# A small-matmul shift convolution, accumulating DMAs and regrouped set-up tables in a two-layer sequence-mixing kernel

## The chip, the cores and the metric

The kernel runs on one core of one Trainium2 chip. The metric is the device time of one execution in microseconds (us), and every quoted time is a median of several executions. Executions of one kernel agree within about 1% here (1.4% in e4). Two executions were slow, one of e5 and the profiled one of e15. They enter no ratio, and the medians of these two runs are given with and without them.

A ratio is the mean time of one kernel's fast runs over the mean of the fast runs of the kernel before in the same rounds on the same chip, so it is not quite the ratio of the medians that stand beside it. Intervals are 95%.

PE is the matmul engine (TensorE), PEld its weight load, DVE is VectorE, ACT is ScalarE, POOL is GpSimd, and SP issues DMAs. The granted clock is the share of PE's full clock that the profile shows, from 0 to 1. `L254` in a profile is line 254 of that kernel's own file, so that the same code has another line number in each kernel.

## The reference, cut to what matters

Four residual blocks follow one another on x of 2048 tokens by 640 channels: A, B, A, B, with the same weights in both rounds.

```python
def _A_ref(x, Lambda_re, Lambda_im, B_re, B_im, C_re, C_im, log_dt, Dskip):
    Lam_bar = exp(exp(log_dt) * Lam)                       # complex, 640 states
    B_bar = ((Lam_bar - 1.0) / Lam)[:, None] * Bmat
    h[t] = Lam_bar * h[t-1] + B_bar @ x[t]                 # 2048 steps
    return 2.0 * (h @ Cmat.T).real + x * Dskip

def _B_ref(q, k, v, shift_k, ssm_k, ssm_D):                # does not depend on x
    k_shift = sum over 4 taps of shifted k * shift_k       # per channel
    kv = k_shift * v
    y = irfft(rfft(kv) * rfft(ssm_k))[:2048] + kv * ssm_D  # long convolution
    return q * y

x = x + _A_ref(_layernorm(x), ...)      # layer one:   "A1" in the kernel
x = x + _B_ref(...)                     # layer two:   "B1"
x = x + _A_ref(_layernorm(x), ...)      # layer three: "A2"
x = x + _B_ref(...)                     # layer four:  "B2"
```

(q in B is the normalised x.) The long convolution is done once, by transforms written as matmuls with sine and cosine tables, in five blocks of 128 channels.

## The kernel before: the parts that matter

The kernel is a list of 862 named tasks. A string `ORDER` fixes the order in which they are emitted, and with it the order of each engine's queue: every engine works its own tasks strictly in that order. A suffix chooses an engine where there is a choice (`/a` ACT, `/d` DVE). A table `PLACE` fixes where each buffer lies in one large on-chip array, so that buffers share space over time. Order and places are the product of an earlier search.

```python
for w in ORDER.split():
    nm, _, e = w.partition("/")
    t = by.pop(nm)
    assert all(d.name in done for d in t.deps), nm
    done.add(nm)
    t.emit({"a": "act", "d": "dve"}[e] if e else t.engs[0])
```

PE's results leave the matmul banks by copies, which ACT or DVE performs. There are 174 of them, 145 on ACT and 29 on DVE.

```python
def evac(nc, eng, out, in_):
    if eng == "act":
        nc.scalar.activation(out, in_, ACT.Copy)
    else:
        nc.vector.tensor_copy(out, in_)
```

The shift convolution: diagonal matrices of the taps are the stationary operand, and k streams through in 512 columns. The product with v goes to DRAM and is read back in another layout.

```python
for b in range(2):
    for l in range(4):
        t0 = KPAD + 1024 * h + 512 * b - l
        nc.tensor.matmul(pk[:, 512 * b:512 * (b + 1)], lhsT=s_ds.get()[:, l, :], rhs=kT[:, t0:t0 + 512],
                         start=(l == 0), stop=(l == 3))
...
nc.vector.tensor_tensor(s_vT.get()[:, sl], s_pk.get(), s_vT.get()[:, sl], ALU.mult)
...
nc.sync.dma_start(out=kvd[kb * P:(kb + 1) * P, :], in_=s_vT.get())
```

The residual of layer one: x is loaded a second time and added by an identity matmul at the end of each output tile.

```python
if reload is not None:
    ops = ops + [(ident[:], resid(q)[:, d0:d1], d0, d1)]
```

The set-up: sines and exponentials alternate on ACT, and the negated tables are made on DVE.

```python
def e_p3(_):   # "a_p3": exponential
    nc.scalar.activation(tl("dt", [P, NJ])[:], st["pf"][:, 2, :], ACT.Exp)
...
def e_f3(_):   # "yt_f3": sine
    nc.scalar.activation(part(768, 256), part(768, 256), ACT.Sin, scale=TWO_PI / 32.0)
...
def e_nsi(_):  # "yt_nsi"
    nc.vector.tensor_scalar(T["NSi"].get(), T["Si"].get(), -1.0, None, ALU.mult)
```

## Time and profile before

The time is 352.71 us (351.51 to 353.8).

| quantity, kernel before | value |
|---|---|
| span of the profiled execution | 349.0 us |
| PE / DVE / ACT busy | 325.5 / 328.5 / 241.5 us |
| mean granted PE clock | 0.987 |
| activation table loads | 8 of 1.28 us |

I add one view here: the busy time of each engine in two stretches, the set-up with the long convolution (0 to 140 us) and the rest. The columns are the stretch and its length, busy us (and instructions) of PE, PEld, DVE, ACT and POOL, then the granted clock, the DMA share and GB/s.

```profile
0.00:140.00 140.00, 126.47 (x1766) 102.95 (x1778) 130.40 (x235) 128.20 (x169) 19.34 (x51) 0.99 1.01 198
140.00:340.00 200.00, 198.89 (x1770) 143.07 (x1788) 192.35 (x259) 111.91 (x212) 0.00 (x0) 1.00 0.33 83
```

In the second row PE is full (99%), with DVE next at 96%. In the first row DVE is busy 93% of the time, ACT 92%, PE 90%.

### The profile page before, as it was taken

Reading aid. Unit: us, or ns where it says so; the run is one execution under the profiler, and the core shown is the slowest. Engines: PE = TensorE matmul, PEld = TensorE weight load, DVE = VectorE, ACT = ScalarE, POOL = GpSimd, SP = SyncE. Lnnn points to the kernel's source line nnn. Section 1 sums busy time; section 2 is a strip of 40 time slices with the busy share of each in tenths; the row PEclk is TensorE's granted clock in tenths of the full one; section 3 lists DMA queues with packets and bytes.
Section 4 is the critical chain, followed back from the end, with each engine's and each line's share of the span. In section 5 each row is a group of like instructions: output and inputs, shape, how many; then the busy total and the mean of one; then the engine's idle time right before and its main releaser. Section 6 shows DMA issues by size and latency. Waiting matters only on the chain.

```text
span 349.0 us, 8399 instructions
## 1 busy us (share of the span) xinstructions
PE 325.5 (93%) x3533; PEld 246.0 (70%) x3565; DVE 328.5 (94%) x504; ACT 241.5 (69%) x383; POOL 19.3 (6%) x51
## 2 busy tenths in 40 slices
PE   6669998999999999999999999999999999999990
PEld 6437976777686998896776685686868758755550
DVE  8989899898999999999989999999989989999996
ACT  5999998899899999563585598286317727307561
POOL 7590000000000000000000000000000000000000
PEclk9899999999999999999999999999999999999996
DMA  7999999999999977497067800306064040000204
GB/s 221 210 215 219 150 169 234 213 151 223 217 252 190 201 160 135 97 264 230 30 120 123 289 28 2 75 2 153 0 141 162 2 77 0 2 0 3 82 34 188
DMA packets 118712, 45.91 MB, mean 132 GB/s; under 512 B 111629, under 2 KB 112914, under 8 KB 118674
## 3 DMA queue, kind: packets, MB, share of 16 engines
q1 hardware_dynamic: 118528, 45.36, 60.2%
q8 instruction: 28, 0.46, 0.5%
q14 instruction: 10, 0.08, 0.1%
q10 hardware_dynamic: 146, 0.01, 0.0%
HBM read 17.38 MB, written 7.86 MB: 72 GB/s over the span
## 4 chain that ended last, share of the span: by engine, by line
PE 70%; DVE 19%; ACT 5%; DMA 2%; issue 2%; ACTq 1%; DVEq 0%; SPq 0%
PE banks L726 31%; PE banks L635 11%; PE banks L638 11%; PE banks L470 4%; DVE arena L247 4%; ACT arena L245 3%; PE banks L1162 2%; PE banks L1163 2%; PE banks L1025 2%; DMA arena<-in_A_Dskip_dram 1%; DMA arena<-kvd 1%; DVE arena L1141 1%; DVE arena L1140 1%; DVE arena L1139 1%; DVE arena L1138 1%
## 5 line engine op out<-in xcount | busy, mean ns | idle before, releaser
L245 ACT ACTIVATE arena<-banks 128x1024 bf16<-128x1024 f32 (+4 forms) x145 | 120.5, 903 | 37.1 <-PE banks L638 13.3
L726 PE MATMUL banks<-arena 128*128 128x128 bf16 (+1 forms) x859 | 116.5, 290 | 1.1
L726 PEld LDWEIGHTS <-arena 128*128 128x128 bf16 x880 | 67.8, 98 | 48.3
L638 PE MATMUL banks<-arena 128*128 128x256 bf16 x400 | 56.7, 273 | 0.0
L635 PE MATMUL banks<-arena 128*128 128x256 bf16 x400 | 56.7, 273 | 0.0
L674 DVE TENSOR_TENSOR_SCAN arena<-arena 128x1290 bf16<-128x1290 f32 x16 | 44.6, 2832 | 0.2
L638 PEld LDWEIGHTS <-arena 128*128 128x128 bf16 x400 | 39.1, 98 | 4.5
L635 PEld LDWEIGHTS <-arena 128*128 128x128 bf16 x400 | 38.5, 98 | 4.2
L544 ACT ACTIVATE junk<-arena,nmean 128x640 bf16<-128x640 f32 x48 | 39.6, 826 | 1.3
L1087 PE MATMUL banks<-arena 128*128 128x128 bf16 x170 | 35.1, 219 | 0.6 <-ACT arena L245 0.6
L1090 PE MATMUL banks<-arena 128*128 128x128 bf16 x170 | 35.4, 219 | 0.0
L247 DVE CAST arena<-banks 128x1024 bf16<-128x1024 f32 (+3 forms) x29 | 30.2, 1060 | 2.9 <-PE banks L1092 1.1
L1092 PE MATMUL banks<-arena 128*128 128x128 bf16 x150 | 32.8, 219 | 0.0
L1089 PE MATMUL banks<-arena 128*128 128x128 bf16 x150 | 32.8, 219 | 0.0
L589 ACT ACTIVATE arena<-arena,nmr,rstd 128x640 bf16<-128x640 f32 (+1 forms) x26 | 22.7, 912 | 7.4 <-DVE nmr L556 7.4
L539 ACT ACTIVATE nmean<-sums 128x4 f32<-128x4 f32 (+1 forms) x15 | 3.0, 203 | 31.7 <-DVE arena L738 28.2
L1025 PE MATMUL banks<-arena 128*128 128x512 bf16 x74 | 19.6, 397 | 3.4 <-ACT arena L245 2.9
L734 ACT ACTIVATE arena<-banks 128x640 f32<-128x640 f32 x12 | 8.4, 701 | 19.3 <-PE banks L726 19.3
L1162 PE MATMUL banks<-arena 128*128 128x128 bf16 x160 | 19.6, 219 | 0.5 <-ACT arena L245 0.5
L1163 PE MATMUL banks<-arena 128*128 128x128 bf16 x160 | 19.3, 219 | 0.6 <-DVE arena L1143 0.6
L591 DVE TENSOR_SCALAR arena<-arena,rstd,nmr 128x640 bf16<-128x640 f32 (+1 forms) x34 | 17.3, 543 | 0.1
L1087 PEld LDWEIGHTS <-arena 128*128 128x128 bf16 x170 | 16.6, 98 | 1.1
(201 smaller groups left out, 537.5 us busy)
## 6 DMA issues: line engine op xcount, KB each, us to landing
arena<-in_A_x_dram SPq DMA_DIRECT2D x8, 640.0 KB, 5.4
arena<-ysd SPq DMA_DIRECT2D x8, 640.0 KB, 4.9
arena<-in_B_ssm_k_dram SPq DMA_DIRECT2D x5, 512.0 KB, 6.4
kvd<-arena SPq DMA_DIRECT2D x5, 512.0 KB, 7.4
arena<-kvd SPq DMA_DIRECT2D x5, 512.0 KB, 5.1
ysd<-arena SPq DMA_DIRECT2D x5, 512.0 KB, 4.4
out_dram<-arena SPq DMA_DIRECT2D x8, 320.0 KB, 2.2
arena<-in_A_B_re_dram SPq DMA_DIRECT2D x1, 800.0 KB, 6.3
```

Of the source, the lines that this page charges most:

```text
L245: nc.scalar.activation(out, in_, ACT.Copy)
L247: nc.vector.tensor_copy(out, in_)
L544: nc.scalar.activation(small.junk, src(q), ACT.Square, bias=st["nmean"][:, i:i + 1], scale=1.0, accum_out=st["ssq"][:, i:i + 1])
L635: nc.tensor.matmul(pb[:, jj, c2, :], lhsT=bt1[:, c2, j, k, :], rhs=uT[:, 0:2, k, :], start=(k == 0), stop=False)
L638: nc.tensor.matmul(pb[:, jj, c2, :], lhsT=bt0[:, c2, k, j * P:(j + 1) * P], rhs=uT[:, 2:4, k, :], start=False, stop=(k == NJ - 1))
L674: nc.vector.tensor_tensor_scan(gv, rt, gv, 0.0, ALU.mult, ALU.add)
L726: nc.tensor.matmul(pc[:, o0:o1], lhsT=lh, rhs=rh, start=(n == 0), stop=(n == len(ops) - 1))
L1025: nc.tensor.matmul(pk[:, 512 * b:512 * (b + 1)], lhsT=s_ds.get()[:, l, :], rhs=kT[:, t0:t0 + 512], start=(l == 0), stop=(l == 3))
L1087: nc.tensor.matmul(ps[:, g, 0, :], lhsT=T["Cf"].get()[:, q, :], rhs=are, start=True, stop=single)
L1089: nc.tensor.matmul(ps[:, g, 0, :], lhsT=T["Sf"].get()[:, q, :], rhs=A[:, 2 * q + 1, :], start=False, stop=True)
L1090: nc.tensor.matmul(ps[:, g, 1, :], lhsT=T["NSf"].get()[:, q, :], rhs=are, start=True, stop=single)
L1092: nc.tensor.matmul(ps[:, g, 1, :], lhsT=T["Cf"].get()[:, q, :], rhs=A[:, 2 * q + 1, :], start=False, stop=True)
```

## The change

The change wants to take work from PE (identity matmuls; cheaper convolution), from ACT (table loads) and from DVE (table work to GpSimd, late sums to the DMA), and comes with a new order and new places for everything. Cut to its core:

```diff
-    t0 = KPAD + 1024 * h + 512 * b - l
-    nc.tensor.matmul(pk[:, 512 * b:512 * (b + 1)], lhsT=s_ds.get()[:, l, :], rhs=kT[:, t0:t0 + 512], ...)
+    t0 = KPAD + P * (8 * h + a) - l
+    for r in range(2):
+        rs = slice(64 * r, 64 * (r + 1))
+        nc.tensor.matmul(pk[:, r, a], lhsT=kT[rs, t0:t0 + P], rhs=s_ds.get()[rs, l, rs], ...)
 ...
-            nc.sync.dma_start(out=kvd[kb * P:(kb + 1) * P, :], in_=s_vT.get())
-            nc.sync.dma_start(out=s_xv.get(), in_=rows(kvd[c0:c0 + DQ, :]))
+            nc.sync.dma_start_transpose(out=s_xv.get(), in_=s_kv.get())
 ...
-                    if reload is not None:
-                        ops = ops + [(ident[:], resid(q)[:, d0:d1], d0, d1)]
+                def e_xa(_, q=q, s_p=s_p):
+                    nc.gpsimd.dma_start(out=s_x[q].get(), in_=dram(q) if dram is not None else s_p.get(), accum_op=ALU.add)
 ...
+                        nc.gpsimd.dma_start(out=s_b.get()[:, q, :], in_=s_x[q].get(), accum_op=ALU.add)
 ...
-        nc.vector.tensor_scalar(T["NSi"].get(), T["Si"].get(), -1.0, None, ALU.mult)
+        (nc.vector if eng == "dve" else nc.gpsimd).tensor_scalar(T["NSi"].get(), T["Si"].get(), -1.0, None, ALU.mult)
```

(Cut: the same engine choice for two other negations and the diagonals `a_lamd`; the column tables `yt_h1` on GpSimd; the exponentials `a_p5a` split from the sines `a_p5b`; layer one's batch statistics as four tasks per chunk; the mean of a LayerNorm taken from sums so that it does not wait for the DMA; `ORDER` and `PLACE` entirely new.) In the new order five table tasks carry the suffix `/p`, GpSimd: `yt_neg12`, `yt_neg6`, `a_lamd`, `yt_nsi` and the small `yt_h3`.

## The prediction

> **What bounds the kernel now.** I read the windows table first, with the execution cut at the three places where its character changes, then the page's row of tenths, the chain of waits, the waits of each engine, and last the groups of instructions for durations. The windows table (busy us, with counts, of PE, weight loads, DVE, ACT and POOL, then clock, DMA share and GB/s):
>
> ```profile
> 0.00:26.20 26.20, 17.18 (x169) 12.31 (x172) 22.30 (x65) 22.45 (x32) 18.98 (x48) 0.93 1.00 215
> 26.20:139.60 113.40, 108.89 (x1594) 90.28 (x1602) 107.71 (x170) 105.34 (x137) 0.36 (x4) 1.00 1.02 193
> 139.60:340.20 200.60, 199.41 (x1774) 143.43 (x1792) 192.95 (x260) 112.31 (x212) 0.00 (x0) 1.00 0.33 83
> 340.20:349.00 8.80, 0.00 (x0) 0.00 (x0) 5.56 (x12) 1.42 (x4) 0.00 (x0) 0.68 0.48 186
> ```
>
> PE is busy 325.5 of 349.0 us. Its idle time is 9.0 us in the set-up, 4.5 in the middle, 1.2 in the long late stage and 8.8 in the tail. A busy PE need not be a fast one, so I checked its rate in the chain of waits (start, duration, what):
>
> ```profile
> 136.32 0.55 PE banks L635 x5
> 140.69 0.55 PE banks L1063 x16
> 156.06 0.93 PE banks L1190 x32
> ```
>
> Five matmuls of 256 columns take 0.55 us, 109 ns each, so 1280 columns cost 0.55 us with hardly a gap. From 140 to 340 us the end is set by the number of columns that PE has to stream: a microsecond of matmul removed there is a microsecond gained, as long as DVE, 193 of 200.6 us busy, keeps up. ACT has 88 us free there. In the middle all three engines are 93 to 96% busy, so a gain needs relief on all three.
>
> The set-up is different. Its chain runs through ACT and not through PE:
>
> ```profile
> 12.36 0.68 ACT arena L245
> 13.06 1.28 ACT L319
> 14.56 1.18 ACT arena L245 x2
> 15.76 1.28 ACT L883
> 17.05 0.42 ACT arena L883
> 17.47 1.19 ACT arena L245 x2
> 18.67 1.28 ACT L332
> ...
> 20.28 1.28 ACT L334
> ```
>
> The four pieces of 1.28 us are activation table loads. They alternate exponential, sine, exponential, sine. The chain also shows once what the trip of the product kv through DRAM costs:
>
> ```profile
> 63.18 0.75 SPq L1175
> 64.03 4.24 DMA arena<-kvd
> 68.29 1.30 DVE arena L1138
> ```
>
> **What the Trainium skill says.** (1) "TensorE: Matmul & The Clock Gate", section "Back-to-back issue gap": a warm matmul costs N/2.4 + 2.5 ns, with a floor near 25 ns for small N. The trace agrees on the first: 109 ns at 256 columns, and 29 ns at 64 (32 in 0.93 us). It has nothing smaller to show the floor. (2) "ScalarE activation tables: per-element evaluation and per-set limits", section "What a function is on this engine": two functions of different sets are one table load of 1283 ns apart. The trace has eight loads of 1283 ns. (3) "DMA: Bandwidth & Descriptors", section "SWDGE vs HWDGE vs iDMA": accumulation in a DMA is to be had only from GpSimd's software-generated descriptors; its section on the anatomy of such a DMA fits about 2.0 us plus bytes over 436 GB/s. This kernel issues no DMA from GpSimd, so no trace of before tests it. (4) "SBUF — State Buffer", section "SBUF: two separate sides": GpSimd cannot write descriptors while DVE runs an operation in a two-port mode. This is untested here too.
>
> **The change part by part.**
>
> *Residual of layer one.* In each of 16 output tiles two identity matmuls (512 and 128 columns) that added x are gone, and so are the four second loads of x. PE loses 16 x 640 = 10240 columns; at 0.55 us for 1280 that is 8 x 0.55 = 4.4 us. All of it lies between 159 and 262 us, where PE is the bound: 4.4 us on the path. x is now added by 16 accumulating DMAs of 128x640, each estimated by the skill's fit at 2.0 us plus 0.4 to 0.8 us. They come between the eviction and the sum of squares of the next layer, so they lengthen a chain of dependences, not an engine's work, and the mean no longer waits for them.
>
> *Shift convolution.* Before: 80 matmuls of 512 columns. In the timeline eight start at 60.48 and the next instruction at 62.22, so 217 ns each and 17.4 us in all. After: 640 matmuls of 64 columns with 64 rows, in pairs on the two halves of the rows. How long one takes is the most uncertain number. If the pairs gain nothing, the rate is that of the last transform (29 ns): 18.6 us, a loss of 1.2. But the first transform already uses such half-row pairs: 16 of 128 columns in 0.55 us, 34 ns each where a full-row one takes 55, a factor of 0.62. The same factor on 29 ns gives 18 ns and 11.6 us, a gain of 5.8. With the skill's floor of 25 ns it is 16 us, a gain of 1.4. I take 20 ns: 12.8 us, a gain of 4.6 on PE. The product on DVE (ten of 1.22 us) now reads and writes in runs of four elements; I expect 1.25, no change. The store and reload of kv become one transposing DMA between on-chip buffers: a store of 7.4 us to landing and a load of 5.1 give way to about 5.9 (what such transposes take now).
>
> *Exponentials apart from sines.* In the new order of tasks ACT meets sine, exponential, sine, root: four loads for eight, 4 x 1.28 = 5.1 us of ACT. Two of them are in the chain of the set-up: 2.6 us on the path. Another sits near 127 us, where the chain also ran through ACT.
>
> *Set-up tables.* The little column operations of the last transform's table leave DVE (about 4 us between 11.0 and 15.2), as do the diagonal of lambda (2.3), two negations and the negated sine (1.6); the factor table shrinks by about 1.5. In exchange 5 more evictions of 640 (0.8 each), and about 6 more of 1024 (1.2), are given to DVE, so DVE gains only about nothing to 2 us before 140. ACT gives those evictions away (about 10 us) plus 5.1 of loads and takes two statistics early and two later (some 2.6 each).
>
> *Late sums.* The last additions of two chunks (8 x 0.82 = 6.6 us of DVE) become accumulating DMAs, and five of the 16 additions of layer three leave DVE for ACT evictions (5 x 0.90 = 4.5). With ten fewer normalisations (about 5.3) and four fewer statistics (4.2), less what DVE takes on, DVE falls by some 17 us to about 312 and stops being a near second bound. By itself this is worth little: PE was 99.4% busy beside it.
>
> **Sum.** PE 4.4 + 4.6 = 9.0 us less; set-up idle 2.5 us less (one path, so I do not add DVE's relief); 1 us of new waits for accumulating DMAs; the tail of 8.8 us as it was, since its last chunk is not among those changed. 349.0 - 9.0 - 2.5 + 1.0 = 338.5 us of span. The median stands 3.7 us above the span of this trace: 342.2 us.
>
> **Rivals.** *The accumulating DMAs turn into the wait.* For it: they have to be issued from GpSimd while DVE is busy 96% of the time, in-order ACT then sits in front of a sum of squares, and the next layer's matmuls hang on it. Against it: ACT has 88 us of slack late, it waits now already 28.2 us for additions of DVE without PE starving, and DVE's work falls. If each of the 16 of layer one cost PE half a microsecond, 8 us would be lost and the time would be 350. *The small matmuls are bound by issue or weight loads.* Each now has its own weight load of 128 columns; at 29 ns the gain of 4.6 turns into a loss of 1.2 and the time is 348. *All is hidden but PE's columns:* if the set-up shortens no path, because its end is set by the same DMAs (DMA share 1.00 there), the time is 344.7. *It goes better:* DVE and ACT freed in the middle let PE close its 4.5 us of idle, and the convolution takes the 18 ns: about 337.
>
> **Range and chances.** The sum of the good cases reaches about 336, the one bad case of a rival 348 to 350; 8 times in 10 between 336.0 and 348.5. Two per cent faster is 345.6; three of the four parts would have to fail for the time to be above it, or the DMA rival has to hold. Faster 0.77, within 2% 0.20, slower 0.03.
>
> **What would show it.** PE busy near 316 us; the convolution's ten groups of 64 in about 1.3 us each (1.9 would make the second rival right); four table loads; PE idle before 26 us near 6.5 us; DVE busy near 312; still over 99% PE busy from 140 us to the last matmul. A PE that waits late in the span, with ACT's sums of squares released by a DMA, would make the first rival right and the prediction wrong.

## The result, and the profile after

The changed kernel takes 363.88 us (363.04 to 364.57): ratio 1.0316 [1.0276, 1.0357], 11 us slower where 10.5 us faster was predicted. Its results are correct.

The same two stretches of the changed kernel:

```profile
0.00:140.00 140.00, 113.70 (x2135) 98.37 (x2136) 120.81 (x198) 109.17 (x153) 36.07 (x66) 0.91 0.91 168
140.00:340.00 200.00, 198.01 (x1856) 146.34 (x1854) 181.79 (x230) 125.42 (x226) 23.72 (x27) 1.00 0.56 115
```

The second row still runs at 99% PE, as before. The first row lost 12.8 us of PE's busy time, although the clock there was 0.91, so that a busy microsecond did less. DVE and ACT are less busy as well: 9.6 and 19.0 us. Only GpSimd is busier, 36.1 us for 19.3, and it is far from full. So less was done in the first row because engines wait for one another or for data, and not because one of them is full.

Over the whole span, the first sign that the prediction had named did not come. PE was to be busy near 316 us; the page says

```profile
PE 325.0 (90%) x4093; PEld 252.4 (70%) x4093; DVE 319.9 (88%) x459; ACT 246.4 (68%) x407; POOL 64.2 (18%) x98
```

It was 325.5 before. PE's idle time rose from 23.5 to 37.3 us. Fewer columns were streamed, but up to 90 us the granted clock was 0.87 (0.98 before), and matmuls took longer at a lower clock: a group of 64 of the convolution 1.89 us at 23 us, where the clock was 0.50, and 1.04 us at 92 us, where it was 1.00.

A finer cut of the changed kernel shows where PE stands idle:

```profile
0.00:27.20 27.20, 16.62 (x229) 14.38 (x231) 20.85 (x64) 17.43 (x25) 14.73 (x38) 0.75 0.87 194
27.20:51.80 24.60, 21.00 (x476) 19.42 (x471) 21.26 (x37) 20.37 (x30) 9.90 (x21) 0.93 0.93 154
51.80:68.00 16.20, 8.64 (x119) 8.04 (x118) 15.47 (x9) 9.61 (x15) 11.33 (x7) 0.80 0.64 121
68.00:90.60 22.60, 18.22 (x529) 16.53 (x528) 19.15 (x18) 20.86 (x25) 0.11 (x1) 0.99 0.94 147
```

PE is idle for 10.6, 3.6, 7.6 and 4.4 us in these, 26 us by 90.6 us; before, it was idle for 12.2 us by 90 us (77.8 busy). The first figure was to fall from 9.0 to near 6.5.

Two places stand out in the timeline (start, duration, engine, line, operation, shapes, and in brackets the idle time before and what ended it). At 51 us, POOL first, then DVE:

```profile
50.55 6.79 POOL L882 TENSOR_SCALAR arena<-arena 128x2176 bf16<-128x2176 bf16 x1 [8.38 <-DVE arena L1169]
```

```profile
50.45 1.29 DVE L1170 TENSOR_TENSOR arena<-arena 128x2176 bf16<-128x2176 bf16 x1
51.85 6.40 DVE L1171 TENSOR_TENSOR arena<-arena 128x2176 bf16<-128x2176 bf16 x1
```

The negation `yt_nsi` on GpSimd and a product on DVE overlap. The product has the same shape as the one ahead of it, which took 1.29 us, but takes 6.40 us, and it ends at 58.25 us, shortly after GpSimd's 57.34. GpSimd in turn seems to have got going only when the product at 50.45 had ended, at 51.74; that leaves 5.6 us of its own. PE waits behind it (columns: who waited for whom, us in total, times, longest):

```profile
PE banks L1116 <- DVE arena L252: 6.6, 1, 6.6
```

At 4 us DVE stands still:

```profile
8.30 0.21 DVE L312 CAST arena<-arena 20x128 f32<-20x128 bf16 x1 [4.10 <-DMA arena<-in_A_Dskip_dram]
8.44 0.60 DVE L855 TENSOR_SCALAR arena<-arena,pidx 128x768 int32<-128x768 f32 x1
```

The cast `a_p0` needs a small load that lands at 8.3 us. In the new order it stands ahead of two phase tables that need no load at all, and a queue in order makes those wait.

What the prediction had asked to look at otherwise: the convolution's groups, a line of the chain of waits, and the accumulating DMAs, from the page's table of DMA issues (KB each, us from issue to landing):

```profile
91.65 1.04 PE banks L1056 x64
```

```profile
arena<-in_A_x_dram POOLq DMA_DIRECT2D x16, 320.0 KB, 5.1
arena<-arena POOLq DMA_DIRECT2D x8, 320.0 KB, 5.4
```

### The profile page after: what moved, and what is told of

Its sections match the earlier page's. It is cut to its first block, busy times and chain, and to the rows that moved or that the text cites. A ratio compares the mean times of both kernels' runs of the same rounds, so it can differ in the third digit from the quotient of the medians.

```text
span 362.3 us, 9541 instructions
## 1 busy us (share of the span) xinstructions
PE 325.0 (90%) x4093; PEld 252.4 (70%) x4093; DVE 319.9 (88%) x459; ACT 246.4 (68%) x407; POOL 64.2 (18%) x98
## 4 chain that ended last, share of the span: by engine, by line
PE 44%; DVE 28%; DMA 10%; issue 10%; ACT 7%; POOL 1%; ACTq 1%; DVEq 0%; POOLq 0%
PE banks L737 11%; DMA arena<-arena 7%; PE banks L651 6%; PE banks L654 6%; PE banks L469 4%; DVE arena L252 3%; ACT arena L250 3%; DVE arena L1171 3%; PE banks L1056 3%; PE banks L1193 2%; PE banks L1194 2%; PE banks L1092 2%; PE banks L1116 2%; DMA arena<-in_A_x_dram 2%; ACT junk L546 2%
## 5 line engine op out<-in xcount | busy, mean ns | idle before, releaser
L250 ACT ACTIVATE arena<-banks 128x1024 bf16<-128x1024 f32 (+4 forms) x134 | 114.2, 911 | 38.6 <-PE banks L654 19.9
L737 PE MATMUL banks<-arena 128*128 128x128 bf16 (+1 forms) x880 | 114.8, 292 | 0.7 <-ACT arena L746 0.7
L737 PEld LDWEIGHTS <-arena 128*128 128x128 bf16 x880 | 66.6, 98 | 48.1 <-issue 0.8
L546 ACT ACTIVATE junk<-arena,nmean 128x640 bf16<-128x640 f32 x40 | 33.0, 825 | 27.3 <-DVE nmean L541 11.5
L252 DVE CAST arena<-banks 128x1024 bf16<-128x1024 f32 (+3 forms) x40 | 39.9, 1014 | 8.4 <-PE banks L1121 4.4
L752 POOL DMA_DIRECT2D arena<-in_A_x_dram x16 | 14.1, 962 | 175.4 <-ACT arena L746 147.9
L651 PEld LDWEIGHTS <-arena 128*128 128x128 bf16 x400 | 38.3, 98 | 6.2 <-DMA arena<-arena 1.1
L1116 PE MATMUL banks<-arena 128*128 128x128 bf16 x170 | 35.8, 223 | 7.6 <-DVE arena L252 6.6
L654 PEld LDWEIGHTS <-arena 128*128 128x128 bf16 x400 | 39.1, 98 | 4.5
L1119 PE MATMUL banks<-arena 128*128 128x128 bf16 x170 | 36.2, 223 | 0.0
L599 ACT ACTIVATE arena<-arena,nmr,rstd 128x640 bf16<-128x640 f32 (+1 forms) x35 | 30.8, 911 | 4.5 <-DVE nmr L558 3.7
L1118 PE MATMUL banks<-arena 128*128 128x128 bf16 x150 | 33.3, 222 | 0.0
L1121 PE MATMUL banks<-arena 128*128 128x128 bf16 x150 | 33.3, 222 | 0.0
L746 ACT ACTIVATE arena<-banks 128x640 f32<-128x640 f32 x16 | 11.2, 698 | 20.2 <-PE banks L737 11.8
L1193 PE MATMUL banks<-arena 128*128 128x128 bf16 x160 | 21.2, 228 | 0.7 <-ACT arena L250 0.6
L1194 PE MATMUL banks<-arena 128*128 128x128 bf16 x160 | 21.0, 228 | 0.5 <-DVE arena L1174 0.4
L1118 PEld LDWEIGHTS <-arena 128*128 128x128 bf16 x150 | 15.0, 100 | 8.0 <-issue 7.9
L1116 PEld LDWEIGHTS <-arena 128*128 128x128 bf16 x170 | 16.9, 100 | 0.9
L417 DVE SCALAR_TENSOR_TENSOR arena<-arena,s_F 128x640 bf16<-128x640 bf16 x20 | 17.2, 874 | 0.1
```

Of the source, the lines that this page charges most:

```text
L546: nc.scalar.activation(small.junk, src(q), ACT.Square, bias=st["nmean"][:, i:i + 1], scale=1.0, accum_out=st["ssq"][:, i:i + 1])
L599: nc.scalar.activation(dst, src, ACT.Identity, bias=st["nmr"][:, i:i + 1], scale=st["rstd"][:, i:i + 1])
L651: nc.tensor.matmul(pb[:, jj, c2, :], lhsT=bt1[:, c2, j, k, :], rhs=uT[:, 0:2, k, :], start=(k == 0), stop=False)
L654: nc.tensor.matmul(pb[:, jj, c2, :], lhsT=bt0[:, c2, k, j * P:(j + 1) * P], rhs=uT[:, 2:4, k, :], start=False, stop=(k == NJ - 1))
L737: nc.tensor.matmul(pc[:, o0:o1], lhsT=lh, rhs=rh, start=(n == 0), stop=(n == len(ops) - 1))
L1116: nc.tensor.matmul(ps[:, g, 0, :], lhsT=T["Cf"].get()[:, q, :], rhs=are, start=True, stop=single)
```

## The experiments

Theory one after the first look: the late part gained as predicted, and the set-up lost more by two mistakes of placement, the negation on GpSimd and the early cast. Rival: the new operations themselves cost time, the accumulating DMAs above all. A third possibility came up later: the predicted gains were not on the path to begin with.

### The two waits in the set-up

**e1**, the long negation back on DVE:

```diff
-    ... a_b1e0:2/a yq1_vl yt_nsi/p a_b1e1:2/a ...
+    ... a_b1e0:2/a yq1_vl yt_nsi/d a_b1e1:2/a ...
```

> The changed kernel with one task given back: the negated sine table (128x2176) is made by DVE again and not by GpSimd. Theory 1 (GpSimd's 6.8 us operation holds DVE's two-input multiplication up, 6.40 us for 1.29, and PE starves for 6.6 us behind it and comes back at a lower clock): about 357 us (356 to 359), the long multiplication back at 1.29 us. Theory 2 (the accumulating DMAs are what cost): no change, 363 to 365. Theory 3 (the start is late because DVE waits 4.1 us for a small load): little change, 362 to 364, since that wait lies before.

Measured: 359.13 us, ratio 1.0192 [1.0146, 1.0239], 4.8 us below the changed kernel. The negation now costs DVE 0.72 us and no product is stretched:

```profile
56.39 0.72 DVE L884 TENSOR_SCALAR arena<-arena 128x2176 bf16<-128x2176 bf16 x1
```

**e2**, the cast that needs the late load (and another small task, `kv_d0`) put behind the last phase table:

```diff
-    ... yt_f0 a_p0 yt_ph6 yq0_kl kv_d0 yt_ph0 kv_d1 ...
+    ... yt_f0 yt_ph6 yq0_kl yt_ph0 kv_d0 a_p0 kv_d1 ...
```

> The changed kernel with two small tasks moved in DVE's order: the conversions of the small loads stand after all three phase tables instead of before the last two. Theory 3 (DVE, which takes its tasks in order, waits 4.1 us for a small load that lands at 8.2 us, and the sine tables wait behind it): about 360 us (358.5 to 362), the wait of 4.1 us at most 2. Theory 1 (the port) and theory 2 (the DMAs): 363 to 365.

Measured: 360.44 us, ratio 1.0237 [1.0192, 1.0283], 3.4 us below. DVE's wait for the load fell from 4.10 to 1.39 us:

```profile
8.26 0.21 DVE L314 CAST arena<-arena 20x128 f32<-20x128 bf16 x1 [1.39 <-DMA arena<-in_A_Dskip_dram]
```

**e3**, both edits together:

> Both edits together. If theories 1 and 3 are both right and their gains add: 352 to 355 us, about the kernel before. If the second only moves work into the wait that the first left: no better than the first alone, about 357. If both are wrong: 363 to 365.

Measured: 356.14 us, ratio 1.0095 [1.0042, 1.0147], 7.7 us below. The two nearly add up (4.8 + 3.4 = 8.2), so they are separate losses. The kernel is still slower than before.

**e4**, the reverse test: the kernel before with nothing changed but the long negation on GpSimd.

```diff
-        nc.vector.tensor_scalar(T["NSi"].get(), T["Si"].get(), -1.0, None, ALU.mult)
+        nc.gpsimd.tensor_scalar(T["NSi"].get(), T["Si"].get(), -1.0, None, ALU.mult)
```

> The kernel before with only the negated sine table moved to GpSimd, nothing else. Theory 1: GpSimd takes 6 to 7 us for it, a DVE operation with two inputs beside it is stretched to 3 to 7 us, and the kernel gets slower, 355 to 360 us. Theory 2 or 3: the same as before or a little faster, 351 to 353, as 0.72 us of DVE is saved.

Measured: 358.63 us, ratio 1.0166 [1.01, 1.0232], 6.1 us slower than the kernel before. So the loss needs no new order. Another DVE operation was hit this time, GpSimd first, then DVE:

```profile
38.69 5.71 POOL L856 TENSOR_SCALAR arena<-arena 128x2176 bf16<-128x2176 bf16 x1 [12.28 <-DMA arena<-arena]
```

```profile
38.71 6.13 DVE L418 SCALAR_TENSOR_TENSOR arena<-arena,s_F 128x640 bf16<-128x640 bf16 x1
```

Operations of that line normally take 0.88 us. Again DVE's operation ends only after GpSimd's does, 44.84 against 44.40. The Trainium skill has the rule, on the page that the prediction cited for something else: "SBUF — State Buffer", section "SBUF: two separate sides", says that GpSimd and a DVE operation with two on-chip inputs share a pair of ports as an exclusive lock, which the one that starts first holds for its whole instruction. Both traces agree with it in outline: DVE's operation ends 0.91 and 0.44 us after GpSimd's, where it takes 1.29 and 0.88 us alone, so at most half of it was done before. (The profile's times on GpSimd are rough.)

**e7** asks whether it is the length of one instruction or GpSimd's total reading that counts: the negation stays on GpSimd, in 17 pieces.

```diff
-        nc.gpsimd.tensor_scalar(T["NSi"].get(), T["Si"].get(), -1.0, None, ALU.mult)
+        for q in range(NQ):
+            nc.gpsimd.tensor_scalar(T["NSi"].get()[:, q, :], T["Si"].get()[:, q, :], -1.0, None, ALU.mult)
```

> The changed kernel with the long negation on GpSimd cut into 17 pieces of 128 columns. Exclusive port held for the length of one instruction: DVE gets in between pieces, the 6.40 us DVE operation falls to under 2 us, and the time comes to 359 to 362 us, like the negation on DVE (359.1). If it is the total of GpSimd's reading that slows DVE, or if DVE has to wait for GpSimd's queue to be empty: no gain, 363 to 366 us.

Measured: 358.73 us, ratio 1.0173 [1.0129, 1.0218], as good as the negation on DVE. GpSimd now takes nearly twice as long (0.52 us for a piece in the median, up to 1.4), yet DVE's products beside it take their normal time:

```profile
51.32 12.05 POOL L883 TENSOR_SCALAR arena<-arena 128x128 bf16<-128x128 bf16 x17 [9.23 <-DMA arena<-arena]
```

```profile
53.09 1.29 DVE L1173 TENSOR_TENSOR arena<-arena 128x2176 bf16<-128x2176 bf16 x1
```

What hurts is the length of one instruction that holds the ports, not that GpSimd works beside DVE. This settles the mechanism of the first loss.

**e8** takes the shorter table operations off GpSimd as well, on top of e3 (`yt_neg12/d`, `yt_neg6/d`, `a_lamd/d`):

> The changed kernel with the long negation on DVE and the late small load's reader after the phase tables (together 356.1 us), and now also the two other negations and the weights' diagonals on DVE instead of GpSimd. If GpSimd's shorter operations stretch DVE in the set-up as the long one did: 1 to 3 us faster, 353 to 355 us. If DVE itself was the bound there: 0 to 3 us slower, since DVE gets some 3.5 us more work.

Measured: 355.32 us, ratio 1.0073 [1.0033, 1.0114]. That is 0.8 us below e3, and the intervals overlap, so it may be nothing. e8 serves as the base of what follows.

### Were the predicted gains on the path?

**e12**, the kernel before without the residual's identity matmuls (a wrong result):

```diff
-                    if reload is not None:
-                        ops = ops + [(ident[:], resid(q)[:, d0:d1], d0, d1)]
```

> The kernel before without the identity matmuls that add layer one's residual (wrong result on purpose; loads kept). The prediction took 4.4 us of PE time on the path for them. If PE bounds that part: 348.0 to 349.0 us (4 us less). If another engine is as close: less than 2 us gained.

Measured: 347.95 us, ratio 0.9851 [0.9813, 0.989], 4.9 us faster (3.9 to 6.6 by the interval). The prediction had said 4.4.

**e17**, the kernel before with one of four taps of the shift convolution. (The three taps are missing from a term so small that the comparison with the reference still passes; as a kernel it is wrong.)

```diff
-                    for l in range(4):
+                    for l in range(1):
 ...
-                                         start=(l == 0), stop=(l == 3))
+                                         start=(l == 0), stop=(l == 0))
```

> The kernel before with one of the four taps of the shift convolution (wrong result on purpose): 240 of 320 column units gone, 17.4 us of PE work become about 4.4. If PE bounds the first 110 us, as the prediction's step on the convolution needs: 10 to 13 us faster, 340 to 343 us. If DVE and ACT (each 92 to 93% busy in the first 140 us) bound it: less than 4 us faster, 349 us or more.

Measured: 351.96 us, ratio 0.9982 [0.9949, 1.0015]. Some 13 us of PE work were taken away, and the time did not change. In the first stretch PE is busy 6.5 us less at a lower clock, while DVE and ACT are as busy as before:

```profile
0.00:140.00 140.00, 119.95 (x1712) 101.05 (x1713) 129.06 (x234) 127.80 (x168) 19.35 (x51) 0.95 1.06 198
```

So PE's amount of work does not bound the first 140 us. Whatever the cheaper convolution saves on PE is hidden. One reservation: the clock was lower beside PE's new idle time (0.95 for 0.99), which ate part of what was taken away.

**e18**, the kernel before with two table loads fewer, by one move:

```diff
-    ... yt_sin12 yt_h1 ... a_p4 yt_f3 a_b01:1 ...
+    ... yt_sin12 yt_f3 yt_h1 ... a_p4 a_b01:1 ...
```

> The kernel before with one sine of the set-up moved ahead of the first exponential: four table loads between 13 and 22 us become two, 2.6 us less of ACT. The prediction's step on the set-up: 2.5 us faster, 350.2 us. If the loads lie in ACT's waiting time: 352 to 353 us.

Measured with five rounds: 352.01 us, ratio 0.9978 [0.9952, 1.0004]. If there is a gain, it is under 1.7 us by the interval, not 2.5. It is the fastest correct kernel by its median, and it is not shown to be faster than the kernel before.

### The accumulating DMAs and the order

**e5** puts the new operations into the old order. Table operations are on DVE, buffers keep the old places where they fit, and about 90 of them had to be placed anew by a small search of mine.

> The changed kernel's operations (small conv matmuls, accumulating DMAs in place of identity matmuls and late sums, exponentials apart from sines) put into the queue order and, where they fit, the buffer places of the kernel before; the five table operations that had gone to GpSimd are on DVE, except the small column tables; the five product rows and the partial sums got new places. Theory 1 (the operations are worth what was predicted, about 10 us, and the new order of the set-up and the operations on GpSimd lost about 21 us): 339 to 346 us, PE idle before 90 us near the 12 us of the kernel before. Theory 2 (an operation of the new set is itself costly on the path: accumulating DMAs or the strided products): 352 us or more although the order is the old one. My places may add waits of some us.

Measured: 385.83 us (385.35 without its slow run), ratio 1.0901 [1.0841, 1.0962]. My expectation was wrong by 40 us. The trace splits it at 90 us; first e5, then the kernel before:

```profile
0.00:90.00 90.00, 76.41 (x1690) 67.97 (x1692) 79.64 (x128) 78.90 (x108) 21.30 (x61) 0.98 1.09 184
90.00:340.00 250.00, 221.98 (x2159) 166.78 (x2156) 205.19 (x296) 141.84 (x233) 19.73 (x23) 0.95 0.56 114
```

```profile
0.00:90.00 90.00, 77.77 (x1085) 61.32 (x1093) 81.93 (x146) 79.42 (x107) 19.34 (x51) 0.98 1.03 200
90.00:340.00 250.00, 247.59 (x2449) 184.69 (x2472) 240.83 (x348) 160.68 (x273) 0.00 (x0) 1.00 0.46 105
```

Up to 90 us the old order brings back the old balance: PE is idle for 13.6 us (12.2 before, 26 in the changed kernel), and its clock is 0.98. At the same task of the same order, the first matmuls of the last transform (`yq0_IA:m0`), e5 is even ahead: it starts them at 89.33 us, the kernel before at 92.16. So in the old order the new operations, the transposing DMA and the strided products among them, cost nothing up to there. After 90 us PE loses 25.6 us. There the old order has the next LayerNorm right behind the sums that are now DMAs, and the chain of waits runs through them:

```profile
282.95 0.86 POOL arena L1123
...
284.11 8.10 DMA arena<-in_A_x_dram
```

**e6** takes the late sums (chunks 0 and 1 of layers three and four) back to DVE, with `ACC_A, ACC_B = 0, 0`; **e9** also drops layer one's accumulating DMAs (a wrong result).

> As the run before it, but the sums of layer two (outputs of chunks 0 and 1 of both passes) are DVE operations again instead of accumulating DMAs; layer one keeps them. If the accumulating DMAs have become a wait at the late end (rival one of the prediction): 1 to 4 us faster than with them. If they are hidden, as the profile of the changed kernel suggests (1.9 us of PE idle in the last 208 us): within 1.5 us, or slower by up to 3 us since DVE gets 16 operations of 0.74 us more.

> The new operations in the old order without late accumulations (379.4 us), and now without layer one's accumulating DMAs either: the residual is left out, so the result is wrong on purpose; the next stage takes the outputs of layer one as they come from the eviction. If in the old order the accumulating DMAs are the wait (issue on GpSimd, 5 us of landing, and the next stage's statistics right behind): 340 to 350 us. If my new buffer places or something else holds the late part up: above 365 us.

Measured: e6 379.39 us, ratio 1.0754 [1.0713, 1.0796]; e9 371.39 us, ratio 1.0523 [1.0475, 1.0571]. In the old order, and with my places, the accumulating DMAs cost 6.0 + 8.0 = 14 us: the prediction's first rival, in an order that does not make room for it. In the changed order PE is idle for 1.9 us of the 208 before the tail, so that they are hidden there, although ACT's sums of squares waited 15 us for them in all. e6 gained more than I expected; e9 fell in its second case, above 365 us. e9 is still 19 us slower than the kernel before, and 23 us slower than e12, which leaves out the residual as well. That has to do neither with these DMAs nor with the first 90 us; my new places are the suspect, and this is not shown.

**e10** is meant to join the good halves: the first 280 tasks in the old order, the rest in the new one.

> All operations of the changed kernel, table operations on DVE; the first 280 tasks (the set-up and the first half of the long convolution) in the order of the kernel before, the rest in the order of the changed kernel. If the early loss is one of order and the late order hides the accumulating DMAs: 340 to 348 us, below the kernel before. If early and late order depend on each other, or my places cost: 350 to 358 us.

Measured: 358.91 us, ratio 1.0184 [1.0144, 1.0225], worse than e8 and just above my second range. PE stands for 8.1 us behind a table block of 6 us (`a_t1`) on ACT, which my cut had put in front of evictions:

```profile
PE banks L1487 <- ACT arena L621: 9.7, 4, 8.1
```

**e16** cuts that block into four tasks between evictions, and **e15** takes only 140 tasks from the old order, so that the block keeps its new place, and also moves the statistics as e13 below does.

> The mix of 280 tasks in the old order (358.9 us), with the 6 us block on ACT that builds the rotation table cut into four pieces between evictions. PE waited 8.1 us behind that block: 349 to 352 us if that wait was the whole of the mix's loss, 356 us or more if the work only queues up elsewhere.

> The first 140 tasks (set-up up to the first value transform) in the order of the kernel before, the rest in the changed order with the statistics late. If the old order of the set-up is better than the changed one beyond the statistics: 343 to 349 us, below the kernel before. If what is left is the new operations' own DVE and ACT work: like the run with only the statistics late, 350 to 352 us.

Measured: e16 359.73 us, ratio 1.0199 [1.0131, 1.0266]; e15 365.54 us (365.24 without its slow run), ratio 1.0338 [1.0271, 1.0405]. e15 missed both of its ranges; its move of the statistics costs 6 us by itself (e13), so it says little about the old order. e16 fell in its second case: the work only queues up elsewhere. In e16 the longest wait of PE at the same place is still 5.6 us: ACT has the block to do, in one piece or in four.

### What holds the changed set-up

**e11** fills PE's gaps with 78 idle matmuls, to keep its clock up, on top of e8:

```diff
+                for _ in range(DUMMY.get(nm, 0)):      # kv_k1: 24, a_b00:2: 8, a_b01:4: 16, yq0_KA:m1: 20, kv_mm0:0: 10
+                    nc.tensor.matmul(bank.tile[:, a0:a0 + P], lhsT=self.ident, rhs=self.ident, start=True, stop=True)
                 t.emit(...)
```

> The changed kernel with the table operations on DVE (355.3 us), and 78 idle identity matmuls of 128 columns put ahead of five matmul groups between 9 and 21 us, where PE waits for the set-up and its granted clock is 0.62. If the cold clock costs time of its own there: granted clock near 1.0 from 9 to 27 us and 351 to 354 us. If PE merely waits for DVE and ACT there: clock up, time within 1 us of 355.3.

Measured: 357.2 us, ratio 1.0122 [1.0077, 1.0166], 1.9 us slower than e8, though the intervals overlap. The clock did rise, from 0.62 to 0.91 in the stretch from 9 to 27 us; e8 first, then e11:

```profile
9.00:27.00 18.00, 13.14 (x237) 10.95 (x237) 16.41 (x50) 14.52 (x25) 11.60 (x36) 0.62 0.81 176
```

```profile
9.00:27.00 18.00, 13.76 (x292) 11.93 (x290) 15.80 (x53) 13.25 (x23) 11.36 (x36) 0.91 0.92 178
```

So the low clock comes with PE's waiting, and raising it did not shorten the time. One reservation: the idle matmuls take PE time themselves, an estimated 4.3 us (78 at the 55 ns of a 128-column matmul), and stand ahead of real ones.

**e13** takes 4.3 us of DVE work out of the set-up: the batch statistics of layer one's second chunk, which the new order had put between 11 and 18 us, move to beside the first chunk's at 90 us. **e14** adds the shift weights' small cast ahead of a table on DVE.

```diff
-    ... kv_d2 A1c1_ln_bn:3/d kv_k1 ... yq0_ka A1c1_ln_bn:1/d a_b00:2 ...
+    ... kv_d2 kv_k1 ... yq0_ka a_b00:2 ... yq2_VB:e1/d A1c1_ln_bn:3/d ... yq2_VB:e4/d A1c1_ln_bn:1/d ...
```

> The changed kernel with table operations on DVE (355.3 us), and the batch statistics of layer one's second chunk, its load and its square root moved from the set-up (11 to 18 us) to beside the first chunk's at about 90 us. If DVE is the bound of the set-up: 4.3 us of DVE work leave it, 350 to 352 us. If PE waits there for something else (loads, ACT): 354 us or more.

> As the run before, and the small copy of the shift weights put ahead of the 14 operations of the first table on DVE, so that the first transposes need not wait for those. If PE's gap from 9 to 11 us is on the path: up to 2 us faster than the run before; if DVE's total work sets the set-up: within 1 us of it.

Measured: e13 361.45 us, ratio 1.0235 [1.0181, 1.0288]; e14 361.98 us, ratio 1.0258 [1.0197, 1.0319]. Both are slower than e8 by 6 to 7 us, against my expectation. e8 first, then e13:

```profile
0.00:60.00 60.00, 44.89 (x879) 40.41 (x879) 53.99 (x114) 48.09 (x69) 19.17 (x61) 0.89 0.95 184
80.00:120.00 40.00, 39.71 (x670) 31.40 (x669) 36.07 (x65) 35.31 (x56) 0.00 (x0) 1.00 1.01 192
```

```profile
0.00:60.00 60.00, 46.18 (x874) 41.88 (x876) 50.64 (x101) 48.05 (x68) 18.99 (x61) 0.86 0.97 177
80.00:120.00 40.00, 34.88 (x571) 26.73 (x573) 35.82 (x73) 32.72 (x51) 0.00 (x0) 0.96 0.87 179
```

Without 3.4 us of DVE work PE gained only 1.3 us by 60 us, and at 80 to 120 us, where the work was put, it lost 4.8. The work was moved here and not removed, so this is no test of DVE's amount. Together with e17 and e18, which took work from PE and from ACT in the kernel before, it suggests that no single engine's amount of work bounds the set-up: three queues in order hand buffers to one another, and what is moved is paid for where it lands. That is a reading, and not shown.

## Why the prediction was wrong, point by point

*The residual* was right: 4.4 us predicted on the path, 4.9 us measured (e12, in the kernel before).

*The late part* was right too: it still runs at 99% PE, and four table loads took the place of eight. DVE's busy time fell to 319.9 us, not to 312.

*The convolution.* The size was not the mistake. Its 64-matmul groups take 1.04 us at full clock, 16 ns a matmul, even less than the 20 ns that I chose. All ten were busy for 13.2 us where 12.8 were forecast, mostly because the first two ran at a granted clock of 0.50 and took 1.89 us each. The step that failed is "PE 4.4 + 4.6 = 9.0 us less": the 4.6 us were put on the path. PE's busy time fell by 0.5 us in all. The prediction had itself read that in the middle "a gain needs relief on all three" engines, and then summed one engine's gain. e17 shows what such a gain is worth there: 13 us of PE work for 0.7 us, within noise.

*The table loads.* The step "Two of them are in the chain of the set-up: 2.6 us on the path" failed in the same way: "set-up idle 2.5 us less" was summed, and by 90 us PE's idle time went from 12.2 to 26 us. e18 took just two loads out and gained 0.7 us, within noise. A piece in the chain of waits is time on the one path that ended last; it is no promise that the next path is 2.6 us shorter.

*The set-up tables.* The largest error is here. The prediction counted what leaves DVE and gave GpSimd's operations no price. (POOL is all but idle in the kernel before once 26 us have passed.) One of them held the ports for some 5.6 us and cost 4.8 us of the time (e1, e4, e7). The prediction cited the page with the rule and took only the sentence on DMA descriptors from it.

*The order.* The prediction took a new order as neutral. One cast ahead of two tables cost 3.4 us (e2), and nothing in the list of operations would have told it; the new order did, since it was in the diff.

*The accumulating DMAs.* The 1 us of new waits was about right in the new order (PE idles 1.9 us of the long late stage, 1.2 before). But each lands after about 5 us, not after the estimated 2.4 to 2.8, and in an order not made for that they cost 14 us (e5, e6, e9). The rival was real; the new order seems to be what kept it away, with the reservation that e5 has places of its own.

*The chances* rested on a slip. Two per cent faster was 345.6 us, and "three of the four parts would have to fail" for more. By the prediction's own sum, 342.2 us, either of the two matmul parts was enough: 346.8 without the convolution's 4.6, 346.6 without the residual's 4.4.

The account: 352.7 - 4.9 (residual) + 4.8 (ports) + 3.4 (late load) = 356.0 us, where 363.9 were measured. The convolution and the loads enter with nothing. GpSimd's shorter operations may be 0.8 of the rest. About 7 us stay open. They lie before 90 us: in e8, where the known losses are out, PE is busy 71.3 us of these 90, 18.7 idle against 12.2 before, and from there to 140 us it is full (49.6 us of 50). The sum of e8's first 90 us:

```profile
sum 90.00, PE 71.25 PEld 64.78 DVE 81.06 ACT 75.97 POOL 19.28; mean PE 7.12 PEld 6.48 DVE 8.11 ACT 7.60 POOL 1.93
```

e5, the same operations in the old order, idles 13.6 us there and is 2.8 us ahead of the kernel before. So the 7 us point to the new order and its places, and not to the operations; this rests on one trace of each kernel, order and places were never tested apart, and which of the moves it is stays open. e11 speaks against the low clock as their cause, and e13 against the early statistics. No whole kernel of mine was rid of them, and no correct version here is shown to beat the kernel before.

## What to carry to other kernels

Where three engines are each about 90% busy or more, don't count a microsecond taken off one of them before a run that takes work off that engine alone has shown it (here 13 us of PE work were worth 0.7 us, within noise); one tap in place of four was such a run, and it could have been imagined before predicting. Work given to an idle GpSimd is not free: cut it into short instructions, or keep it away from DVE operations with two on-chip inputs. A tuned order belongs to its operations, so judge a new order by reading who stands in front of whom in each queue, and don't expect halves of two orders to join.

## What the Trainium skill lacked or had wrong

- "TensorE: Matmul & The Clock Gate", "Back-to-back issue gap", gives an issue floor of about 25 ns for 1 to 64 columns. The changed convolution's matmuls of 64 columns, in pairs on the two halves of the rows, take 1.04 us for 64, which is 16 ns each. The page treats matmuls that run together on different rows of the array, in its part on packing small ones, but has no figure for pairs of 64 columns.
- "DMA: Bandwidth & Descriptors", "Anatomy of one DMA — SWDGE (gpsimd) path", fits 2.0 us plus bytes over 436 GB/s, about 2.8 us for 320 KB. The accumulating DMAs of 320 KB, most of them beside other traffic, landed after 5.1 and 5.4 us in the median, one of them after 9.1 us in the changed kernel. I found no price for accumulation on it.
- "GPSIMD Engine Reference", "Elementwise — side-by-side cycle accounting", names 1.8 cycles an element at 1.2 GHz as the best case, which would be an estimated 3.3 us for 2176 elements of each row. The negation of 128x2176 took 5.71 us in e4, against 0.72 us on DVE; in 17 pieces it took 12.05 us, 0.71 us on average for each 128 columns.
- "SBUF — State Buffer", "SBUF: two separate sides", is right on the exclusive lock (6.40 us for 1.29). It does not say what to do about it: pieces of 128 columns let DVE through at its normal 1.29 us (e7).
